# Query projection of a two-head attention step on all 128 rows, and the keys' last tokens as a block diagonal

## The chip, the cores and the metric

The kernel runs as one program on one core of a Trainium2 chip. The metric is the device time of one execution in microseconds (us). A difference of up to 0.2% (2.9 us) between two kernels is about what a measurement of this kernel can't tell from no change.

## What is computed

Three stages follow one another. The first is an attention with a feature map: `phi` projects queries and keys with one 64x128 matrix, subtracts the largest absolute value of the row, and takes `exp` of plus and of minus the result.

```
def phi(x):
    proj = np.einsum('bhsd,df->bhsf', x, w_phi)
    proj = proj - np.max(np.abs(proj), axis=-1, keepdims=True)
    return np.concatenate([np.exp(proj), np.exp(-proj)], axis=-1)
q_p, k_p = (phi(q), phi(k))
kv = np.einsum('bhsf,bhsd->bhfd', k_p, v)
z = np.sum(k_p, axis=2)
num = np.einsum('bhsf,bhfd->bhsd', q_p, kv)
den = np.einsum('bhsf,bhf->bhs', q_p, z)[..., None] + 1e-06
return (num / den).astype(np.float32)
```

There are 4 batches, 8 heads, 576 tokens and 64 numbers per head. The second stage is `g @ w_out` with `g = h - tanh(h)` and `h = x @ w_in` (2304 tokens, 512 to 2048 to 512). The third adds four experts, `out += p[:, e] * (relu(x @ w1[e]) @ w2[e])`, 512 to 1024 to 512.

## The kernel before, in words

**Split numbers.** Most large products take each fp32 operand as a high and a low part of type fp32r. `split3` (L371 holds its matmul) issues three matmuls for each product: high by high, high by low and low by high.

**Order.** For the first two stages nothing is issued directly. `add` (class `Issue`) records a node with an engine, an assumed duration, the nodes that it waits for, the buffers and PSUM banks that it takes, and a due time. `Issue.run` then plays these nodes through once, with the assumed durations, and issues them in the order that comes out. A node's assumed duration, its buffers and its banks therefore decide where its instructions, and those of its neighbours, stand on each engine. On the chip every engine works through its own list in order. The third stage is in an order written by hand.

**Attention tasks.** Two heads are worked on together: head 0 of the pair lies on partitions 0 to 63, head 1 on 64 to 127. There are 16 key tasks (`k_task`: 4 batches by 4 pairs) and 32 query tasks (`q_task`: each with half of the tokens, N = 288). They lie in the first 410 us or so, mixed with the second stage's blocks (`moe_slot`, `moe_x2`) of 288 tokens.

**Query task.** Three transposes (L541) bring 288 tokens of both heads into one PSUM bank. ScalarE copies that to the high part `qh` (L544), VectorE subtracts to the low part `ql` (L545). Then six matmuls (L555) project: for each of three pairs of weight and data (`wph` by `qh`, `wph` by `ql`, `wpl` by `qh`) one matmul for each head. Each uses 64 rows of the array; the two heads' matmuls of a pair write different banks. `wph` and `wpl` hold the 64x128 matrix twice, one copy under the other.

**Key task.** Four transposes (L428) and one more for the last 64 tokens (L431, from `krawr`, of which only partitions 0 to 63 hold data). ScalarE copies 512 tokens to `kT` (L434), VectorE the last 64 tokens (L436). Eight fp32 matmuls on 64 rows project the 512 tokens (L447), and two fp32 matmuls on 64 rows and 64 columns (`mmr`, L465) the last ones. L497, L501 and L507 are the products of key features with `v` and with ones; they write 64 partitions at a time.

**Names used later.** L581 transposes a query task's projection (`pq`) for the maximum, L597 multiplies its exponentials by `kv`, L612 transposes its result. L511 transposes a key task's sums. L648 to L653 are the second stage's activation. L319 to L328 convert the second stage's weights from 64-bit words.

## Time and profile before

| what | value |
|---|---|
| median of three executions | 1437.89 us (1437.07 to 1438.95) |
| span of the profiled execution, first to last instruction | 1435.3 us |
| TensorE busy / its weight loads | 98% / 89% of the span |
| VectorE, ScalarE, GpSimd busy | 75%, 47%, 47% |
| mean granted TensorE clock | 0.995 |

The span is 2.6 us under the median of the executions; what lies around it is start and end of the program. "PE" is TensorE's matmuls and "PEld" its weight loads, "DVE" VectorE, "ACT" ScalarE, "POOL" GpSimd, "SP" the engine whose queue issues the loads and stores. Matmuls are pipelined: one matmul of 288 columns is shown as some 0.29 us long, while the next starts 0.13 us after it. What a matmul takes from TensorE is the distance from its start to the start of the next; a busy share near 100% hides gaps shorter than that overlap.

### The profile page before, as it was taken

To read this page: it belongs to the slowest core of one execution; us is meant where nothing else is said; L and a number is where in the kernel's file an instruction comes from. 1 tells how busy PE (TensorE), PEld (TensorE's weight loads), DVE (VectorE), ACT (ScalarE), POOL (GpSimd) and SP (SyncE) were. 2 spreads that over 40 slices of the span, in tenths; PEclk is the share of its full clock that TensorE was granted. 3 is DMA by queue.
4 is the path that set the end of the run, shared out by engine and by line. 5 is a ranking of instruction groups with operands and counts; after the bars stand their busy time and mean duration, and the time that the engine had idled before them with its cause. 6 is when DMAs were issued, how large, how long until landed. Compare 5 with 4: busy or idle time off the path is not lost.

```text
span 1435.3 us, 24190 instructions
## 1 busy us (share of the span) xinstructions
PE 1401.6 (98%) x9088; PEld 1278.5 (89%) x9088; DVE 1074.9 (75%) x1943; ACT 677.8 (47%) x1639; POOL 677.8 (47%) x567
## 2 busy tenths in 40 slices
PE   8988999999999999999999999999999999999998
PEld 6777888989999999999889999898999989999997
DVE  5898578888867866766777777877777788777774
ACT  6756566666656655564433333433333343333331
POOL 2786354554414322254545544654454466445441
PEclk9999999999999999999999999999999999999999
DMA  6531225443414333212232121233222123221211
GB/s 175 168 114 56 83 88 153 131 131 105 136 52 165 118 132 111 93 74 88 78 103 74 59 73 62 71 118 97 72 67 74 60 74 111 66 73 60 74 44 44
DMA packets 118339, 133.77 MB, mean 93 GB/s; under 512 B 49232, under 2 KB 90320, under 8 KB 118224
## 3 DMA queue, kind: packets, MB, share of 16 engines
q1 hardware_dynamic: 118064, 132.18, 28.7%
q8 instruction: 71, 1.16, 0.3%
q14 instruction: 44, 0.36, 0.1%
q10 hardware_dynamic: 160, 0.07, 0.0%
HBM read 104.44 MB, written 27.79 MB: 92 GB/s over the span
## 4 chain that ended last, share of the span: by engine, by line
PE 83%; DVE 6%; POOL 3%; issue 3%; ACT 3%; DMA 1%; SPq 1%; POOLq 0%; DVEq 0%; ACTq 0%
PE acc L371 36%; PE bank L371 35%; PE bank L597 3%; PE bank L497 1%; POOL wslot L328 1%; PE bank L581 1%; PE bank L555 1%; DVE hs L650 1%; PE acc L497 1%; DVE xc L992 1%; PE bank L447 1%; PE acc L507 1%; DMA xq<-x2f 1%; DVE th L652 0%; DVE wtmp L814 0%
## 5 line engine op out<-in xcount | busy, mean ns | idle before, releaser
L818 POOL TENSOR_TENSOR wslot<-wtmp,wslot 128x512 fp32r<-128x512 f32 x96 | 124.3, 1295 | 268.9 <-ACT wslot L816 166.3
L371 PE MATMUL acc<-gh,wslot 128*128 128x288 f32 x1024 | 240.5, 304 | 3.2 <-ACT gh L653 3.0
L371 PEld LDWEIGHTS acc<-gh,wslot 128*128 128x128 f32 x1024 | 174.7, 189 | 8.1 <-issue 4.0
L964 POOL TENSOR_TENSOR wslot<-raw,wslot 128x512 fp32r<-128x512 f32 x96 | 137.7, 1454 | 91.2 <-ACT wslot L964 88.6
L246 POOL TENSOR_TENSOR gl<-th,gh 128x288 fp32r<-128x288 f32 x92 | 81.2, 883 | 180.0 <-ACT gh L653 151.0
L371 PE MATMUL acc<-gl,wslot 128*128 128x288 f32 x512 | 151.8, 296 | 1.0 <-POOL gl L246 1.0
L652 DVE COPY_PREDICATED th<-sq,hs 128x288 f32<-128x288 int32 x128 | 86.5, 677 | 47.4 <-ACT sq L651 47.2
L371 PE MATMUL bank<-xt0h,wslot 128*128 128x288 f32 x496 | 112.0, 301 | 4.0 <-POOL wslot L328 2.4
L371 PE MATMUL bank<-xt1h,wslot 128*128 128x288 f32 x512 | 114.0, 298 | 0.2 <-DVE kd L454 0.2
L818 POOL TENSOR_TENSOR wslot<-raw,wslot 128x512 fp32r<-128x512 f32 x96 | 109.0, 1154 | 4.4 <-ACT wslot L816 4.4
L992 DVE TENSOR_TENSOR xc<-bank,xc 128x384 f32<-128x384 f32 x168 | 92.2, 549 | 11.6 <-PE bank L371 11.6
L992 DVE TENSOR_TENSOR xc<-acc,xc 128x384 f32<-128x384 f32 x168 | 92.1, 549 | 11.3 <-PE acc L371 10.6
L371 PEld LDWEIGHTS acc<-gl,wslot 128*128 128x128 f32 x512 | 97.0, 189 | 1.2 <-POOL gl L246 1.2
L814 DVE TENSOR_TENSOR wtmp<-raw 128x256 f32<-128x256 f32 x96 | 96.8, 1008 | 0.0
L651 ACT ACTIVATE sq<-sq,b_m 128x288 f32<-128x288 f32 x128 | 69.0, 540 | 47.9 <-DVE hs L650 45.6
L371 PEld LDWEIGHTS bank<-xt0h,wslot 128*128 128x128 f32 x496 | 83.5, 189 | 6.1 <-POOL wslot L328 3.3
L648 DVE SCALAR_TENSOR_TENSOR hs<-bank,sq 128x288 f32<-128x288 f32 x126 | 57.0, 453 | 41.9 <-ACT th L647 40.7
L653 ACT ACTIVATE gh<-th 128x288 fp32r<-128x288 f32 x128 | 57.4, 448 | 62.8 <-PE acc L371 37.5
L371 PEld LDWEIGHTS bank<-xt1h,wslot 128*128 128x128 f32 x512 | 86.0, 189 | 1.1 <-DVE kd L454 0.4
L646 ACT ACTIVATE sq<-bank 128x288 f32<-128x288 f32 x126 | 51.8, 411 | 61.9 <-PE bank L371 59.8
L650 DVE SCALAR_TENSOR_TENSOR hs<-sq,hs 128x288 f32<-128x288 f32 x128 | 76.6, 599 | 0.0
L371 PE MATMUL bank<-xt1l,wslot 128*128 128x288 f32 x256 | 75.8, 296 | 0.0
(397 smaller groups left out, 4097.1 us busy)
## 6 DMA issues: line engine op xcount, KB each, us to landing
raw<-in_moe_w_dram SPq DMA_DIRECT2D x96, 512.0 KB, 3.6
raw<-in_moe_w_in_dram SPq DMA_DIRECT2D x16, 512.0 KB, 4.4
raw<-in_moe_w_out_dram SPq DMA_DIRECT2D x16, 512.0 KB, 5.3
qraw<-in_q_dram SPq DMA_DIRECT2D x32, 144.0 KB, 2.9
x2s<-x2p SPq DMA_DIRECT2D x8, 576.0 KB, 3.3
x2p<-x2s SPq DMA_DIRECT2D x8, 576.0 KB, 6.2
x2f<-x2p SPq DMA_DIRECT2D x8, 576.0 KB, 2.8
out_dram<-yacc SPq DMA_DIRECT2D x18, 256.0 KB, 2.1
```

Source lines behind the costliest of these rows:

```text
L246: return add("POOL", c_pool(n), lambda: POOL.tensor_tensor(out=o, in0=a, in1=b, op=op), deps, due, bufs)
L371: PE.matmul(ps, lhsT=a, rhs=b, start=start and n == 1, stop=stop and n == 3 * len(pairs))
L646: x1 = add("ACT", c_act(N, True), lambda: ACT.activation(out=sq.t, in_=at(bk)[:, 0:N], func=ACTF.Square), [a], due, [sq], frees=[bk])
L648: y1 = add("DVE", c_dve(N), lambda: DVE.scalar_tensor_tensor(out=hs.t, in0=at(bk)[:, 0:N], scalar=P1, in1=sq.t, op0=ALU.mult, op1=ALU.mult ...
L650: y3 = add("DVE", c_dve(N), lambda: DVE.scalar_tensor_tensor(out=hs.t, in0=sq.t, scalar=P0 / P1, in1=hs.t, op0=ALU.add, op1=ALU.mult), [y1 ...
L651: x3 = add("ACT", c_act(N, ptr=True), lambda: ACT.activation(out=sq.t, in_=sq.t, func=ACTF.Relu, scale=-1.0, bias=b_m[:, 0:1]), [y3], due ...
L652: y4 = add("DVE", c_dve(N), lambda: DVE.copy_predicated(out=th.t, mask=sq.t.bitcast(I32), data=hs.t), [x3, y2, y3], due + 1.4, [th, sq, hs])
L653: x4 = add("ACT", c_act(N), lambda: ACT.activation(out=gh.t, in_=th.t, func=ACTF.Copy), [y4], due + 2, [th, gh])
L814: steps = [("DVE", 0.36, lambda o=o, a=a, b=b, op=op: DVE.tensor_tensor(out=o, in0=a, in1=b, op=op)) for o, a, b, op in sums]
L818: steps.append(("POOL", c_pool(n), lambda h=h, l=l, src=src: POOL.tensor_tensor(out=l, in0=src, in1=f32(h), op=ALU.subtract)))
L964: todo2 = [lambda c=c: (ACT.activation(out=vh[:, c], in_=r2[:, c], func=ACTF.Copy), POOL.tensor_tensor(out=vl[:, c], in0=r2[:, c], in1=f32 ...
L992: DVE.tensor_tensor(out=o, in0=bk, in1=a, op=ALU.add)
```

## The change

Each head of the query task now has its own 128-row operand: on one half of the partitions its high part, on the other half its low part. Two matmuls on all 128 rows for each head (with `wph`, then `wpl`, accumulated) give four terms, low by low among them. The copy and the subtraction are done for each head apart, on 64 partitions of output, and each head's projection is a node of its own with one bank. In the key task, the last 64 tokens of the two heads are loaded by two transfers into the diagonal blocks of `krawr`, so that one fp32 matmul on 128 rows by 128 columns projects both; the transposed block has a buffer of its own, `kTr`.

```diff
-        DVE.memset(t[64:128], 0.0)
+        DVE.memset(t[0:64, 1], 0.0)
+        DVE.memset(t[64:128, 0], 0.0)
...
-    kT_r = ring(att, 1, [128, S], F32, "kT")
+    kT_r = ring(att, 1, [128, 512], F32, "kT")
+    kTr_r = ring(att, 1, [128, 128], F32, "kTr")
...
-    qh_r = ring(att, 2, [128, N], F32R, "qh")
-    ql_r = ring(att, 2, [128, N], F32R, "ql")
+    qx_r = ring(att, 2, [128, 2, N], F32R, "qx")
...
-            (rrb.t[0:64], k[b, h:h + 2, 512:S, :].rearrange("h p d -> p h d")),
+            (rrb.t[0:64, 0], k[b, h, 512:S, :]),
+            (rrb.t[64:128, 1], k[b, h + 1, 512:S, :]),
...
-        a2 = add("DVE", c_dve(64), lambda: DVE.tensor_copy(out=kT.t[:, 512:S], in_=at(bb)[:, 0:64]), [a], t0 + 0.6, [kT], frees=[bb])
+        a2 = add("DVE", c_dve(128), lambda: DVE.tensor_copy(out=kTr.t, in_=at(bb)[:, 0:128]), [a], t0 + 0.6, [kTr], frees=[bb])
...
-            for e in range(2):
-                h0 = 64 * e
-                PE.matmul(at(bk)[h0:h0 + 64, 0:128], lhsT=kT.t[h0:h0 + 64, 512:S], rhs=wphi[h0:h0 + 64, :], start=True, stop=True)
+            PE.matmul(at(bk)[:, 0:128], lhsT=kTr.t, rhs=wphi, start=True, stop=True)
...
-        a = add("PE", 0.41, mmr, [a2], due, [kT, kdr], bank=bk)
+        a = add("PE", 0.3, mmr, [a2], due, [kTr, kdr], bank=bk)
...
-        a1 = add("ACT", c_act(N, True), lambda: ACT.activation(out=qh.t, in_=at(bk)[:, 0:N], func=ACTF.Copy), [a], t0 + 0.5, [qh], frees=[bk])
-        a1 = add("DVE", c_dve(N), lambda: DVE.tensor_tensor(out=ql.t, in0=at(bk)[:, 0:N], in1=f32(qh.t), op=ALU.subtract), [a1], t0 + 0.9, [qh, ql], frees=[bk])
...
-        def proj():
-            for n, (w, x) in enumerate(((wph, qh), (wph, ql), (wpl, qh))):
-                for e in range(2):
-                    h0 = 64 * e
-                    PE.matmul(at(pb[e])[:, 0:N], lhsT=w[h0:h0 + 64, :], rhs=x.t[h0:h0 + 64, :], start=n == 0, stop=n == 2)
-
-        a = add("PE", 0.42, proj, [a1], t0 + 1.4, [qh, ql, pq, ea, eb], banks=pb)
+        pj = []
+        for e in range(2):
+            own, other = slice(64 * e, 64 * e + 64), slice(64 - 64 * e, 128 - 64 * e)
+
+            def proj(e=e):
+                for n, w in enumerate((wph, wpl)):
+                    PE.matmul(at(pb[e])[:, 0:N], lhsT=w, rhs=qx.t[:, e], start=n == 0, stop=n == 1)
+
+            a = add("ACT", c_act(N, True), lambda e=e, own=own: ACT.activation(out=qx.t[own, e], in_=at(bk)[own, 0:N], func=ACTF.Copy), [tr_done], t0 + 0.5, [qx], frees=[bk])
+            a = add("DVE", c_dve(N), lambda e=e, own=own, other=other: DVE.tensor_tensor(out=qx.t[other, e], in0=at(bk)[own, 0:N], in1=f32(qx.t[own, e]), op=ALU.subtract), [a], t0 + 0.9, [qx], frees=[bk])
+            pj.append(add("PE", 0.28, proj, [a], t0 + 1.4, [qx, pq, ea, eb], bank=pb[e]))
```

The copy of the projection (`pq`) and the exponentials then wait for their own head's projection instead of for both.

**How the order moves, TensorE in the steady part.** This is the last query task, about 409 us into the run before, between two products of the second stage (`bank<-xt...` is the first layer, `acc<-g...` the second). Before:

```order
L371 MATMUL bank_87<-xt0l,wslot_126 128x288
L371 MATMUL bank_87<-xt0h,wslot_126 128x288
L555 MATMUL bank_86<-qh_217,wph 128x288
L555 MATMUL bank_85<-qh_217,wph 128x288
L555 MATMUL bank_86<-ql_219,wph 128x288
L555 MATMUL bank_85<-ql_219,wph 128x288
L555 MATMUL bank_86<-qh_217,wpl 128x288
L555 MATMUL bank_85<-qh_217,wpl 128x288
L371 MATMUL acc_80<-gh_257,wslot_131 128x288
L371 MATMUL acc_80<-gl_261,wslot_131 128x288
```

The same place on TensorE after the change (L613 is the transpose that was L612):

```order
L371 MATMUL bank_85<-xt0l,wslot_126 128x288
L371 MATMUL bank_85<-xt0h,wslot_126 128x288
L554 MATMUL bank_87<-qx_220,wph 128x288
L554 MATMUL bank_87<-qx_220,wpl 128x288
L371 MATMUL acc_80<-gh_258,wslot_131 128x288
L371 MATMUL acc_80<-gl_262,wslot_131 128x288
L371 MATMUL acc_80<-gh_258,wslot_131 128x288
L613 MATMUL bank_86<-ident,xf_235 128x96 x3
L554 MATMUL bank_84<-qx_220,wph 128x288
L554 MATMUL bank_84<-qx_220,wpl 128x288
L371 MATMUL acc_81<-gh_258,wslot_131 128x288
```

Six matmuls in one piece became two pieces of two, one for each head, with other work between them.

**VectorE at the start.** The first key and query task, 6 to 10 us into the run. Before (L453 and L454 are the keys' maximum and its subtraction):

```order
L378 MEMSET krawr_190 64x128
L378 MEMSET krawr_191 64x128
L436 COPY kT_196<-acc_82 128x64
L545 TENSOR_TENSOR ql_218<-acc_81,qh_216 128x288
L453 TENSOR_REDUCE km_200<-acc_83 128x4
L453 TENSOR_REDUCE km_200<-acc_80 128x4
```

After the change (L455 is the maximum that was L453):

```order
L378 MEMSET krawr_191 64x64
L379 MEMSET krawr_191 64x64
L438 COPY kTr_199<-acc_82 128x128
L557 TENSOR_TENSOR qx_219<-acc_81,qx_219 64x288 x2
L455 TENSOR_REDUCE km_203<-acc_83 128x4
L455 TENSOR_REDUCE km_203<-acc_80 128x4
```

Ahead of the first maximum stand two subtractions in place of one, and a copy of twice the width.

**TensorE at the start.** The stretch before the first product of keys and `v` (L497), 10 to 14 us into the run. Before:

```order
L581 MATMUL bank_87<-ident,pq_220 96x128 x3
L581 MATMUL acc_82<-ident,pq_220 96x128 x3
L431 MATMUL acc_83<-ident,krawr_191 128x128
L541 MATMUL acc_81<-ident,qraw_194 128x96 x3
L497 MATMUL acc_80<-kp_202,vbuf_98 64x256
```

After (the rows L449, the second key task's projection, come eight times in all):

```order
L541 MATMUL acc_82<-ident,qraw_197 128x96 x3
L582 MATMUL bank_87<-ident,pq_221 96x128 x3
L433 MATMUL acc_81<-ident,krawr_191 128x128
L449 MATMUL acc_83<-wphi,kT_198 128x128
L449 MATMUL acc_80<-wphi,kT_198 128x128
...
L497 MATMUL acc_81<-kp_205,vbuf_98 64x256
```

The transposes of the third query load no longer stand ahead of L497; the second key task's projection does, which stood behind L507 before.

## Rows read from the trace of the kernel before

**Rows 1.** Windows: stretch, its length, busy of each engine, PEclk, DMA share, GB/s.

```profile
0.00:50.00 50.00, 45.11 (x412) 35.74 (x412) 30.93 (x79) 32.80 (x89) 18.38 (x18) 0.97 0.62 162
50.00:140.00 90.00, 77.62 (x647) 67.55 (x648) 82.31 (x151) 57.70 (x159) 69.15 (x57) 0.96 0.38 113
140.00:410.00 270.00, 267.26 (x2356) 241.84 (x2355) 208.05 (x452) 171.62 (x496) 128.35 (x125) 1.00 0.36 111
120.00:125.00 5.00, 3.15 (x12) 2.94 (x13) 5.00 (x9) 1.68 (x3) 2.79 (x3) 0.73 0.02 5
500.00:650.00 150.00, 150.00 (x1131) 150.00 (x1130) 102.56 (x217) 81.67 (x192) 49.09 (x50) 1.00 0.27 98
```

**Rows 2.** Chain that ended last, shares by line: 50 to 140, then 140 to 410 us.

```profile
by line: issue 14.2%; PE bank L371 8.2%; POOL wtmp L319 5.8%; POOL gl L246 5.8%; DVE th L652 4.2%; POOL wslot L328 4.1%; DVE hs L650 4.0%; DVE kd L454 3.5%; DVE km L453 3.4%; PE acc L371 3.3%; PE acc L497 2.7%; POOL xf L607 2.6%; PE acc L50
...
by line: PE acc L371 22.6%; PE bank L371 19.5%; PE bank L597 16.0%; PE bank L497 7.7%; PE bank L581 4.6%; PE bank L555 4.2%; PE bank L447 3.3%; DVE hs L650 2.2%; PE bank L612 1.9%; PE bank L541 1.9%; PE bank L511 1.6%; PE bank L501 1.4%; PE
```

**Rows 3.** Timeline of PE at 409 us: start, length, engine, line, op, tiles, form, count.

```profile
409.00 0.29 PE L371 MATMUL bank<-xt0h,wslot 128*128 128x288 f32 x1
409.22 0.40 PE L555 MATMUL bank<-qh,wph 64*128 64x288 f32 x2
409.45 0.29 PE L555 MATMUL bank<-ql,wph 64*128 64x288 f32 x2
409.59 0.29 PE L555 MATMUL bank<-qh,wpl 64*128 64x288 f32 x2
409.81 0.40 PE L371 MATMUL acc<-gh,wslot 128*128 128x288 f32 x1
410.05 0.29 PE L371 MATMUL acc<-gl,wslot 128*128 128x288 f32 x1
```

**Rows 4.** Timeline of PE at 113 us: transposes between two L371.

```profile
112.73 0.30 PE L371 MATMUL acc<-gh,wslot 128*128 128x288 f32 x1
112.86 0.41 PE L541 MATMUL bank<-ident,qraw 96*128 96x96 f32 x3
113.06 0.38 PE L371 MATMUL acc<-gh,wslot 128*128 128x288 f32 x1
113.28 0.29 PE L371 MATMUL acc<-gl,wslot 128*128 128x288 f32 x1
```

**Rows 5.** Chain in order of time: start, us, what, count.

```profile
19.84 1.09 PE acc L447 x16
...
22.11 0.37 PE bank L465 x4
...
33.53 0.44 PE acc L511 x4
...
500.68 1.60 PE bank L371 x12
```

**Rows 6.** Windows, busy (count): VectorE in L545; last row TensorE, loads in L555.

```profile
0.00:50.00 50.00, 2.27 (x5) 0.97 0.62 162
50.00:140.00 90.00, 3.14 (x7) 0.96 0.38 113
140.00:410.00 270.00, 8.80 (x20) 1.00 0.36 111
...
140.00:410.00 270.00, 14.70 (x132) 9.59 (x132) 1.00 0.36 111
```

**Rows 7.** Chain in order of time, near 132 and near 66 us.

```profile
131.96 0.36 DVE xt0l L628
...
65.51 0.60 ACT pq L561 x2
```

**Rows 8.** Timeline of PE near 121 us; in brackets idle time before, releaser.

```profile
120.89 0.40 PE L371 MATMUL acc<-gh,wslot 128*128 128x288 f32 x1 [2.97 <-ACT gh L653]
```

**Rows 9.** Timeline: the SP queue's second load, and PE's wait near 13 us.

```profile
1.54 0.76 SPq L254 DMA_DIRECT2D krawr<-in_k_dram  x1
...
13.55 0.71 PE L541 MATMUL acc<-ident,qraw 96*128 96x96 f32 x3 [2.57 <-DMA qraw<-in_q_dram]
```

More of the change, by code (lines that the diff above doesn't have):

```diff
@@ L422, in k_task @@
         ], due=t0 - 4, bufs=[vb])
-        kT, km = kT_r.take(), km_r.take()
+        kT, kTr, km = kT_r.take(), kTr_r.take(), km_r.take()
         ba, bb = Bank(), Bank()
@@ L434, in k_task @@
         a1 = add("ACT", c_act(512, True), lambda: ACT.activation(out=kT.t[:, 0:512], in_=at(ba), func=ACTF.Copy), [a], t0 + 0.5, [kT], frees=[ba])
-        a = add("PE", 0.1, trr, [ld], t0 + 0.1, [rrb, kT], bank=bb)
-        a2 = add("DVE", c_dve(64), lambda: DVE.tensor_copy(out=kT.t[:, 512:S], in_=at(bb)[:, 0:64]), [a], t0 + 0.6, [kT], frees=[bb])
+        a = add("PE", 0.1, trr, [ld], t0 + 0.1, [rrb, kTr], bank=bb)
+        a2 = add("DVE", c_dve(128), lambda: DVE.tensor_copy(out=kTr.t, in_=at(bb)[:, 0:128]), [a], t0 + 0.6, [kTr], frees=[bb])
         kps, es = [], []
@@ L536, in q_task @@
         ], due=t0 - 8, bufs=[rb])
-        bk, qh, ql = Bank(), qh_r.take(), ql_r.take()
+        bk, qx = Bank(), qx_r.take()
         def tr():
@@ L541, in tr @@
                 PE.transpose(out=at(bk)[:, r * QP:(r + 1) * QP], in_=rb.t[:, r].rearrange("p h d -> p (h d)"), identity=ident[0:QP, 0:QP])
-        a = add("PE", 0.3, tr, [ld], t0, [rb, qh, ql], bank=bk)
-        a1 = add("ACT", c_act(N, True), lambda: ACT.activation(out=qh.t, in_=at(bk)[:, 0:N], func=ACTF.Copy), [a], t0 + 0.5, [qh], frees=[bk])
-        a1 = add("DVE", c_dve(N), lambda: DVE.tensor_tensor(out=ql.t, in0=at(bk)[:, 0:N], in1=f32(qh.t), op=ALU.subtract), [a1], t0 + 0.9, [qh, ql], frees=[bk])
+        tr_done = add("PE", 0.3, tr, [ld], t0, [rb, qx], bank=bk)
         pb = [Bank(), Bank()]
         pq, ea, eb = pq_r.take(), ea_r.take(), eb_r.take()
-        def proj():
-            for n, (w, x) in enumerate(((wph, qh), (wph, ql), (wpl, qh))):
-                for e in range(2):
-                    h0 = 64 * e
-                    PE.matmul(at(pb[e])[:, 0:N], lhsT=w[h0:h0 + 64, :], rhs=x.t[h0:h0 + 64, :], start=n == 0, stop=n == 2)
-        a = add("PE", 0.42, proj, [a1], t0 + 1.4, [qh, ql, pq, ea, eb], banks=pb)
+        pj = []
[7 more added lines that the diff above has]
+            pj.append(add("PE", 0.28, proj, [a], t0 + 1.4, [qx, pq, ea, eb], bank=pb[e]))
         pc, xe = [None, None], []
@@ L560, in copy @@
             def copy(e=e):
-                pc[e] = add("ACT", c_act(N, True), lambda: ACT.activation(out=pq.t[:, e], in_=at(pb[e])[:, 0:N], func=ACTF.Copy), [a], t0 + 2, [pq], frees=[pb[e]])
+                pc[e] = add("ACT", c_act(N, True), lambda: ACT.activation(out=pq.t[:, e], in_=at(pb[e])[:, 0:N], func=ACTF.Copy), [pj[e]], t0 + 2, [pq], frees=[pb[e]])
             def exps(e=e):
                 for x, sg in ((ea, 1.0), (eb, -1.0)):
-                    xe.append(add("ACT", c_act(N, True), lambda x=x, sg=sg: ACT.activation(out=x.t[:, e], in_=at(pb[e])[:, 0:N], func=ACTF.Exp, scale=sg), [a], t0 + 2.4, [x], frees=[pb[e]]))
+                    xe.append(add("ACT", c_act(N, True), lambda x=x, sg=sg: ACT.activation(out=x.t[:, e], in_=at(pb[e])[:, 0:N], func=ACTF.Exp, scale=sg), [pj[e]], t0 + 2.4, [x], frees=[pb[e]]))
             copy()
```

## Prediction
> **What bounds the kernel now.** I read the windows first, since attention, where every edited line runs, lies in the first 410 us. [rows 1] give three regimes. From 140 to 410 us TensorE is busy 267.3 of 270 us, VectorE 208.1 (77%), ScalarE 171.6. From 50 to 140 us VectorE is busy 82.3 of 90 us (91%) and TensorE 77.6. From 0 to 50 us neither is full. From 500 to 650 us, after attention, TensorE is busy all 150 us, so what attention saves is not waited for again there.
>
> The chain of work that ended last says the same by line [rows 2]. From 140 to 410 us it runs along TensorE: the three largest entries are L371, L371 and L597, and the query projection itself (L555) has 4.2%. From 50 to 140 us it is scattered over TensorE, GpSimd, VectorE and 14.2% of time between engines; no line has more than a tenth. So a slot of TensorE saved after 140 us should come back nearly whole; before that it should come back only in part, and VectorE work may cost.
>
> **TensorE: what a query projection takes now.** Not the 0.29 us of a row counts, but the distance between starts. Twelve L371 in a row take 1.60 us [rows 5]: 0.133 us is the plain slot of 288 columns. In [rows 3] the projection's two matmuls of a pair start together (x2 in each row): the two heads do run beside each other. But the group stands out at both ends. From the last L371 to the first pair are 0.22 us in place of 0.133, and from the first to the second pair 0.23 in place of 0.133; the next step is 0.14. On the way back it is 0.22 from the last pair to L371, and 0.24 to the L371 behind. So each passage between whole-array and 64-row matmuls costs about 0.09 at the boundary and 0.10 to 0.11 for weights that are not loaded ahead, 0.197 us together. From 409.00 to 410.05 the group takes 1.05 us, where two slots of L371 would take 0.27: it costs 0.78 us.
>
> Is it the 64-row form that costs, or any change of work? [rows 4] show three transposes (L541) between two L371: they start 0.13 after the L371 ahead, and the L371 behind is followed after 0.22. So whole-array work of another kind has no boundary cost going in, and something like 0.09 coming back from fp32. The projection after the change is fp32r like L371 and uses the whole array, so I take nothing at its ends.
>
> The Trainium skill (TensorEngine Tiling (Array Packing), Key Properties) says that a change of tiling mode drains TensorE, and that tiles work independently. The 0.22 against 0.133 at both ends agrees; the second 0.10 is not in that sentence.
>
> **TensorE: what it takes after.** Four matmuls on 128 rows: 4 x 0.133 = 0.53 us, in one piece or in two. Against 0.78 that is 0.25 less where both neighbours use the whole array. The general count comes from the order: walking down TensorE's whole list, the form changes (all rows; 64 rows; 64 columns, L497 to L507; 64 by 64, L465) 141 times before and 62 times after, 79 fewer. At 0.197 that is 15.6 us; at 0.15, since L465 loads only 64 columns and some neighbours are fp32, 11.9 us. The extra streaming is one slot for each of 32 query tasks (three pairs become four matmuls): 32 x 0.133 = 4.3 us. For L465 [rows 5], four records (two heads, two passes) take 0.37 us with its exit; after the change one fp32 matmul of 128 columns has two passes, by the nearest row (L511, four of 128 columns in 0.44, 0.11 each) 0.22 us. Its streaming is thus unchanged, its switches are in the 79. Sum for TensorE: 11.9 - 4.3 = 7.6 to 15.6 - 4.3 = 11.3 us less; I take 9.5.
>
> Where does it fall? 20 of 32 low-part subtractions (L545) stand after 140 us, 7 between 50 and 140, 5 before [rows 6]. Of the six matmuls of each of 32 tasks, 132 of 192 follow 140 us [rows 6], those of 22 tasks. So 22/32 x 9.5 = 6.5 us are saved where TensorE is the chain; I count it whole. The other 3.0 lie before 140 us.
>
> **VectorE and ScalarE: what is added.** Instead of one subtraction on 128 partitions there are two on 64, each with the same 288 columns. No 64-partition subtraction of this form is in the trace; below, it could take half, above, the whole of a 128-partition one. I take the whole, for what is passed through is columns. In the chain such a subtraction holds VectorE 0.36 us (L628, [rows 7]), so 32 x 0.36 = 11.5 us, of which 20 x 0.36 = 7.2 after 140 us and 7 x 0.36 = 2.5 between 50 and 140. The copy of the keys' last tokens doubles to 128 columns: 64 more at 0.36/288 are 0.08 us each, 1.3 for 16 tasks. ScalarE gets 32 more copies; two of that size take 0.60 in the chain [rows 7], so 32 x 0.30 = 9.6 us.
>
> After 140 us both are covered: VectorE has 62 us idle there, ScalarE 98, and TensorE's own stream is the cover. If that cover is gone in a piece (VectorE full for some 10 us), the subtractions of one or two tasks show, 0.36 to 0.7 us. Between 50 and 140 us VectorE is nearly full, so 2.5 + 6 x 0.08 = 3.0 us can show; bounds 0 and 3.0, and I take 1.8, towards the upper end because 91% is nearer to full than not.
>
> **Latency.** Head 0's operand is ready as before (one copy, one subtraction), head 1's one step of 0.36 later; its TensorE node is apart, so the list can hold other work between them, as the steady place in the order shows. What waits behind a late head 1 is the rest of TensorE's list, but at most 0.36 us.
>
> **The start.** The second `krawr` transfer costs the SP queue about 0.76 us [rows 9] in each key task; ahead of the second query load stand two of them, so it lands some 1.5 us later. Ahead of the first key maximum VectorE gets one more subtraction and two more small memsets, 0.5 to 0.7 us. Against that, before, TensorE stands 2.57 us at the transposes of the third query load [rows 9], and behind them waits L497. In the new order these transposes no longer precede L497; the second key projection (L449, sixteen records, 1.09 us [rows 5]) does, and it is done early. What is late next is L497 itself, for its exponentials. I take 1 us gained by 50 us, between a loss of 1.5 and a gain of 3.
>
> **Sum.** -6.5 (after 140 us) + 1.8 (VectorE, 50 to 140) - 1.0 (start) = -5.7 us. From the span 1435.3 that gives 1429.6, and with the 2.6 us that lie around it 1432.2; the median shown is 1437.9. The forecast is 1432.2 us.
>
> **Rivals.**
>
> *VectorE takes it.* TensorE's saving is real, but in parts of the stretch after 140 us too a block's end waits for VectorE, and only the rest of it pays. For it: the 91%, and `hs` L650 is the only entry of another engine among the first eight of the chain after 140 us. Against: there TensorE idles 2.7 of 270 us. The 6.5 shrink to about 4, all of VectorE's 3.0 shows and the start brings nothing: -1.0, 1436.9 us.
>
> *The pairs were worth more than the switches.* If the 0.197 at the ends is not of the form but of the waits that surround any group, it stays, and the change only turns three slots into four. 4.3 us more on TensorE give 1442.2 us, with VectorE's 3.0 on top 1445.2. It decides as soon as less than 4.3/79 = 0.054 us is saved per switch. Against: the 0.22 is the same where the transposes have none [rows 4]. The Trainium skill speaks for it (TensorEngine Tiling (Array Packing), Theoretical Speedup): a contraction of up to 64 gains up to 2x by row tiles. By that rule alone, without the switches, the time would be the 1442.2 us of this rival; the x2 rows agree that pairs run together, the ends say that the doubling is not what these groups got.
>
> *A long wait in the new order.* Before 140 us the whole list is shuffled. Near 121 us TensorE stands 2.97 us [rows 8], and over 120 to 125 us its granted clock is 0.73 on the mean [rows 1]: part of that stretch ran at the lower level of 1.2 GHz, which costs 0.27 x 5 = 1.35 us more. One event of this kind costs 4.3 us. TensorE's idle time before 140 us is 4.9 + 12.4 = 17.3 us [rows 1], so there is room for the new order to be luckier or unluckier. Two more such events turn the forecast into 1440.8 us; shedding the present one gives 1427.9.
>
> **Chances.** The forecast's mechanism with a gain between 3 and 10 us: 0.57. The same with waits shed too, about 1428: 0.09. VectorE takes it, within 0.2%: 0.20. Pairs worth more: 0.06, slower. Waits in the new order, slower: 0.08. That gives faster 0.66, same 0.20, slower 0.14. The range runs from 1425 (the present event shed, and TensorE's upper sum: 22/32 x 11.3 = 7.8 in place of 6.5, a start of -2.5 in place of -1) to 1440.5 us (nearly two added events); for the forecast alone it is 1428 to 1435.
>
> **What the profile after would show.** L554 in starts 0.13 us apart with 0.13 at both ends if the form is the cause; 0.22 there if it is not. L465 followed by 0.11 steps. In the window that answers to 140 to 410 us, the same second-stage products ending about 6 us earlier with TensorE still near full. VectorE near 0.36 us for each L557, or half of that if partitions count. The prediction is wrong if TensorE's idle time before 140 us grows past 20 us, if more stretches show a clock near 0.7, or if the 64-partition subtraction that writes other partitions than it reads takes much longer than the old one.

## The result and the profile after

The change made the kernel slower: 1451.59 us (median of four, 1450.64 to 1453.92) against 1438.42 us of the kernel before on the same chip (1437.07 to 1439.89). The ratio is 1.0087, 95% interval 1.0073 to 1.0101, some 12.5 us. The forecast was 1432.2 us. The profiled execution has a span of 1449.9 us.

The windows after, which answer to [rows 1] (same columns; the third reaches to 426 us, since attention now ends later, the fourth is a part of the second):

```profile
0.00:50.00 50.00, 44.70 (x400) 38.37 (x402) 34.87 (x86) 34.87 (x95) 14.66 (x17) 0.97 0.58 154
50.00:140.00 90.00, 76.62 (x596) 67.44 (x593) 80.04 (x149) 57.53 (x155) 62.42 (x52) 0.91 0.37 114
140.00:426.00 286.00, 274.25 (x2359) 251.60 (x2358) 227.64 (x487) 188.49 (x540) 131.01 (x130) 1.00 0.34 105
...
69.20:76.20 7.00, 7.00 (x46) 6.65 (x45) 4.68 (x12) 2.69 (x9) 6.03 (x6) 0.51 0.89 289
...
500.00:650.00 150.00, 150.00 (x1131) 150.00 (x1131) 101.14 (x216) 81.88 (x193) 50.14 (x52) 1.00 0.27 98
```

From 500 to 650 us TensorE is as full as before (150 of 150 us). After 140 us TensorE now stands for 286 - 274.25 = 11.8 us, before for 2.7. From 50 to 140 us its mean granted clock is 0.91 where it was 0.96, which is 0.05 x 90 = 4.5 us of its time; from 69.20 to 76.20 us it ran at the lower level (0.51 of full) while it was busy all the time.

A block of the second stage ends with four copies from `acc` to `x2p`. The tile's view (line, count, durations in ns, first and last start in us) of before and of after, for the first six of eight blocks:

```profile
L710 ACT ACTIVATE x2p<-acc x24: 387/452/513, 144.0 to 413.1; 128x288 f32<-128x288 f32 x24
```

```profile
L711 ACT ACTIVATE x2p<-acc x24: 392/412/541, 140.6 to 424.7; 128x288 f32<-128x288 f32 x24
```

The same view for all eight blocks:

```profile
L710 ACT ACTIVATE x2p<-acc x32: 387/430/513, 144.0 to 476.0; 128x288 f32<-128x288 f32 x32
```

```profile
L711 ACT ACTIVATE x2p<-acc x32: 388/412/541, 140.6 to 488.1; 128x288 f32<-128x288 f32 x32
```

The two profiled spans differ by 14.6 us. The sixth block ends 11.6 us later and the eighth 12.1, so most of the loss lies in the stretch with attention. The other 2.5 us fall behind the eighth block, where no edited line runs; there the time differs between the runs below, too, from 959 to 967 us. The first and last start of the six blocks serve for the experiments.

The timeline of TensorE after, at a place where the operand is in time, answers to [rows 3]:

```profile
208.72 0.29 PE L371 MATMUL acc<-gh,wslot 128*128 128x288 f32 x1
208.85 0.29 PE L554 MATMUL bank<-qx,wph 128*128 128x288 f32 x1
208.98 0.29 PE L554 MATMUL bank<-qx,wpl 128*128 128x288 f32 x1
209.12 0.30 PE L371 MATMUL bank<-xt0h,wslot 128*128 128x288 f32 x1
```

Every step is 0.13 us: no boundary, no exposed weights. So the part of the forecast on TensorE's own time holds here. What it did not see is in the waits after 140 us (engine, line, what it waited for, us in total, times, longest):

```profile
PE acc L371 <- ACT x2p L711: 3.0, 2, 2.3
PE bank L554 <- DVE qx L557: 2.8, 3, 1.5
PE bank L433 <- DVE xt1l L629: 1.5, 1, 1.5
PE bank L613 <- DVE qx L557: 1.4, 1, 1.4
```

TensorE waits for the new subtractions (L557), and for copies on ScalarE that stand behind the new ones. Two of these waits, in the timelines of GpSimd, VectorE and TensorE near 348 us, then of VectorE, GpSimd, ScalarE and TensorE near 371 us:

```profile
347.55 0.74 POOL L484 TENSOR_TENSOR ks<-ks,kpr 64x256 f32<-64x256 f32 x1
348.25 1.30 POOL L481 TENSOR_TENSOR tz<-kp 128x512 f32<-128x512 f32 x1
...
347.65 2.24 DVE L653 COPY_PREDICATED th<-sq,hs 128x288 f32<-128x288 int32 x1
349.93 0.46 DVE L557 TENSOR_TENSOR qx<-bank,qx 64x288 fp32r<-64x288 f32 x1
...
350.53 0.44 PE L613 MATMUL bank<-ident,xf 96*128 96x96 f32 x3 [1.42 <-DVE qx L557]
351.02 0.37 PE L554 MATMUL bank<-qx,wph 128*128 128x288 f32 x1
```

```profile
369.06 0.95 DVE L320 TENSOR_SCALAR wtmp<-wtmp 128x512 uint32<-128x512 uint32 x1
...
369.94 2.28 DVE L653 COPY_PREDICATED th<-sq,hs 128x288 f32<-128x288 int32 x1
...
370.57 1.30 POOL L481 TENSOR_TENSOR tz<-kp 128x512 f32<-128x512 f32 x1
...
372.25 0.45 DVE L557 TENSOR_TENSOR qx<-bank,qx 64x288 fp32r<-64x288 f32 x1
...
372.25 0.44 ACT L654 ACTIVATE gh<-th 128x288 fp32r<-128x288 f32 x1 [2.06 <-DVE th L653]
372.74 0.83 ACT L556 ACTIVATE qx<-bank 64x288 fp32r<-64x288 f32 x2
373.47 1.28 ACT L711 ACTIVATE x2p<-acc 128x288 f32<-128x288 f32 x4
...
373.92 0.40 PE L371 MATMUL acc<-gh,wslot 128*128 128x288 f32 x1 [2.29 <-ACT x2p L711]
```

Both begin with L653, which lasts 2.24 and 2.28 us in place of some 0.5 while GpSimd sums key features (L484, L481). Behind it come a subtraction, or ScalarE's list with two new copies in it, and TensorE stands still for 1.42 and 2.29 us.

### The profile page after: what moved, and what is told of

It is laid out like the page before. It is cut to its first block, busy times and chain, and to the rows that moved or that the text cites. A ratio compares the mean times of both kernels' runs of the same rounds, so it can differ in the third digit from the quotient of the medians.

```text
span 1449.9 us, 24098 instructions
## 1 busy us (share of the span) xinstructions
PE 1402.0 (97%) x8992; PEld 1285.1 (89%) x8992; DVE 1094.6 (75%) x1977; ACT 693.1 (48%) x1671; POOL 669.7 (46%) x567
## 4 chain that ended last, share of the span: by engine, by line
PE 81%; DVE 8%; issue 3%; ACT 3%; POOL 2%; DMA 2%; SPq 1%; POOLq 0%; DVEq 0%; ACTq 0%
PE bank L371 35%; PE acc L371 34%; PE bank L598 3%; POOL wslot L328 1%; PE bank L497 1%; PE bank L582 1%; PE bank L554 1%; DVE wtmp L322 1%; DVE hs L651 1%; PE acc L598 1%; PE bank L449 1%; DMA xq<-x2f 1%; DVE xc L993 1%; PE acc L497 1%; DVE th L653 1%
## 5 line engine op out<-in xcount | busy, mean ns | idle before, releaser
L371 PE MATMUL acc<-gh,wslot 128*128 128x288 f32 x1024 | 241.1, 301 | 3.3 <-ACT x2p L711 3.3
L371 PEld LDWEIGHTS acc<-gh,wslot 128*128 128x128 f32 x1024 | 175.0, 188 | 4.5 <-ACT x2p L711 4.3
L371 PE MATMUL acc<-gl,wslot 128*128 128x288 f32 x512 | 151.3, 295 | 1.8 <-POOL gl L246 0.9
L653 DVE COPY_PREDICATED th<-sq,hs 128x288 f32<-128x288 int32 x128 | 87.1, 681 | 49.6 <-ACT sq L652 49.4
L371 PE MATMUL bank<-xt0h,wslot 128*128 128x288 f32 x496 | 113.3, 303 | 6.6 <-POOL wslot L328 4.2
L371 PE MATMUL bank<-xt1h,wslot 128*128 128x288 f32 x512 | 113.5, 296 | 0.3 <-DVE th L650 0.3
L993 DVE TENSOR_TENSOR xc<-bank,xc 128x384 f32<-128x384 f32 x168 | 92.3, 549 | 11.6 <-PE bank L371 11.5
L371 PEld LDWEIGHTS acc<-gl,wslot 128*128 128x128 f32 x512 | 96.5, 189 | 2.7 <-POOL gl L246 1.5
L371 PEld LDWEIGHTS bank<-xt0h,wslot 128*128 128x128 f32 x496 | 84.5, 191 | 9.5 <-POOL wslot L328 5.4
L371 PEld LDWEIGHTS bank<-xt1h,wslot 128*128 128x128 f32 x512 | 85.6, 188 | 0.8 <-DVE th L650 0.5
L371 PE MATMUL bank<-xt1l,wslot 128*128 128x288 f32 x256 | 75.5, 295 | 0.0
## 6 DMA issues: line engine op xcount, KB each, us to landing
qraw<-in_q_dram SPq DMA_DIRECT2D x32, 144.0 KB, 2.9
```

Source lines behind the costliest of these rows:

```text
L371: PE.matmul(ps, lhsT=a, rhs=b, start=start and n == 1, stop=stop and n == 3 * len(pairs))
L653: y4 = add("DVE", c_dve(N), lambda: DVE.copy_predicated(out=th.t, mask=sq.t.bitcast(I32), data=hs.t), [x3, y2, y3], due + 1.4, [th, sq, hs])
L993: DVE.tensor_tensor(out=o, in0=bk, in1=a, op=ALU.add)
```

## Experiments

Four theories were put to the test. **A**: split by heads, the operand's links copy, subtraction, copy, subtraction stand one behind the other, and TensorE waits. **T** (called C in the first expectations): 32 more operations on VectorE and on ScalarE are too much in themselves. **B**: any change of the plan's numbers draws another order, with other waits and other stretches at half clock. **D**: the new passes, or the keys' third transfer, don't pay. Each ratio is to the kernel before on the same chip, with its 95% interval. "Stretch" is the distance from the first `x2p` copy to the last in the tile's view, 413.1 - 144.0 = 269.1 us before; it leaves out what happens ahead of the first copy, and is given where the order is the old one. Both columns come from the one execution that was profiled, whose time is up to some 3 us off the median of its kernel, so a first copy alone that is 2 or 3 us later shows little.

| run | order | ratio (95%) | first copy, stretch |
|---|---|---|---|
| the change | its own | 1.0087 (1.0073 to 1.0101) | - |
| e1 new keys only | its own | 1.0050 (1.0038 to 1.0062) | - |
| e2 new query only | its own | 1.0064 (1.0046 to 1.0082) | - |
| e3 whole change, unsplit | old | 1.0047 (1.0035 to 1.0060) | 147.4, 272.2 |
| e5 whole change, unsplit | its own | 1.0031 (1.0019 to 1.0042) | - |
| e6 before | e5's | 0.9998 (0.9988 to 1.0007) | - |
| e7 passes only | old | 1.0003 (0.9990 to 1.0015) | 148.1, 264.2 |
| e8 work only | old | 1.0054 (1.0038 to 1.0070) | 145.1, 276.8 |
| e9 before | e1's | 1.0042 (1.0029 to 1.0056) | - |
| e10 work, not waited for | old | 1.0026 (1.0017 to 1.0035) | 145.4, 273.0 |
| e11 subtraction only | old | 1.0050 (1.0038 to 1.0063) | 147.5, 276.5 |
| e12 new keys only | old | 1.0004 (0.9995 to 1.0013) | 146.0, 267.4 |
| e14 the change, copies first | the change's | 1.0069 (1.0056 to 1.0081) | - |
| e15 before, no sums | old | 0.9940 (0.9927 to 0.9952) | 139.8, 265.1 |
| e16 work only, no sums | old | 0.9965 (0.9953 to 0.9977) | 144.0, 268.1 |
| e17 whole change, no sums | old | 0.9962 (0.9949 to 0.9974) | 144.8, 263.6 |
| e18 new keys, third load moved | old | 0.9989 (0.9980 to 0.9997) | 146.8, 267.4 |
| e19 whole change, chained | old | 1.0120 (1.0102 to 1.0137) | 151.5, 277.0 |
| e20 e18, key copy on ScalarE | old | 0.9994 (0.9984 to 1.0003) | 148.8, 267.1 |

"Old order" means that nodes and assumed durations are those of before and that only what a node issues differs, so that on every engine the instructions stand in the old order. (In e19 the second copy is issued with the subtractions, and so stands later in ScalarE's list; in e20 a copy changes its engine.)

**e1 and e2: the halves of the change.** e1 takes the parts of the diff on `krawr`, `kT`, `kTr` and `mmr`, e2 the parts on `qx`.

> The block diagonal of the keys' last tokens alone; the query projection is the old one. Theory A (the time was lost in the query step: its links copy, subtraction, copy, subtraction stand one behind the other, so that TensorE waits for head 1): the keys' part is free of that, so 1434 to 1438 us (16 groups of two 64-row matmuls become one whole-array pair of passes, at most 16 x 0.2 = 3.2 us less TensorE, part of it before 140 us where VectorE bounds). Theory B (any change of the planner's numbers reshuffles the order of the first 140 us, and it is the order that loses or wins): the order changes here too, so a time off the kernel before by more than 4 us either way is likely. Theory C (the additional copies and subtractions are too much for ScalarE and VectorE): none here, as A.

> The query projection of the change, split by heads, with the old keys. Theory A: most of the loss is here, 1444 to 1452 us. Theory B: yet another order, anywhere from 1434 to 1452, with idle time before 140 us and half clock that set it.

1447.93 and 1449.48 us: each half alone loses, and the two losses do not add up. Theory A had said that the keys alone are free of the loss, and it missed; e1 is off by more than 4 us, as theory B had it, and e2 fits both. That called for a fixed order.

**e3, e5 and e6: one node for both heads, in the old order and in its own; the old instructions in the latter.**

```diff
+        def halves():
+            for e in range(2):
+                own = slice(64 * e, 64 * e + 64)
+                ACT.activation(out=qx.t[own, e], in_=at(bk)[own, 0:N], func=ACTF.Copy)
...
-        a1 = add("ACT", c_act(N, True), lambda: ACT.activation(out=qh.t, in_=at(bk)[:, 0:N], func=ACTF.Copy), [a], t0 + 0.5, [qh], frees=[bk])
+        a1 = add("ACT", c_act(N, True), halves, [a], t0 + 0.5, [qx], frees=[bk])
```

(the subtractions and the four matmuls alike; e5 with `2 * c_act`, `2 * c_dve` and 0.56.)

> The instructions of the whole change (block-diagonal keys, stacked operands, four whole-array query matmuls), but a pair's two copies are one step of the plan, its two subtractions one step and its four matmuls one step, with the plan's durations as before: the order on every engine is that of the kernel before. Theory A: the links copy, subtraction, copy, subtraction are gone (both copies first, then both subtractions), head 1 comes some 0.8 us later than before (one copy 0.39, one subtraction 0.45) and most places have that slack: 1429 to 1436 us. Theory B: the order is the old one, so the old idle time stays and the saving on TensorE shows: 1429 to 1433. Theory C: the work is all here, so the loss stays: 1445 to 1452.

> As the kernel with the old order, but the plan knows the true durations (two copies, two subtractions, 0.56 us of matmuls, 0.3 us of key matmul), so the order is a new one. Theory A: no chain from head to head, 1429 to 1436 us. Theory B: another draw of the order, anywhere from 1428 to 1452, and not the time of the kernel with the old order. Theory C: 1445 to 1452.

> The instructions of the kernel before (64-row matmuls, one copy, one subtraction) in exactly the order of the unsplit kernel with true durations. Theory B: the order sets the time, so it differs from the kernel before by as much as the unsplit kernel does, give or take the 5 to 9 us of TensorE that the instructions are worth. Theory A: the order alone costs little, 1436 to 1441 us. Theory C: 1436 to 1441 us, and 8 us or more faster than the unsplit kernel, since the additional work is left out.

1446.71, 1445.63 and 1439.49 us. Theories A (1429 to 1436 us) and B (1429 to 1433) missed e3, and A missed e5. With the order held the instructions still lose 0.47%; in another order they lose about 0.33% (1.0031 against 0.9998), and that order is worth nothing by itself, against theory B. So the loss is not only the order's, and it is there without a split by heads.

**e7, e8, e11: the parts of e3 apart.** e7 has the whole-array passes and leaves out the additional work, so each head's matmuls read high parts or low parts of both heads; e8 has the additional work with the old matmuls (the copies are cut like the subtractions shown); e11 is as e8 with the copy whole.

```diff
 # e7
-            for e in range(2):
-                own = slice(64 * e, 64 * e + 64)
-                ACT.activation(out=qx.t[own, e], in_=at(bk)[own, 0:N], func=ACTF.Copy)
+            ACT.activation(out=qx.t[:, 0], in_=at(bk)[:, 0:N], func=ACTF.Copy)
 # e8
-            DVE.tensor_tensor(out=ql.t, in0=at(bk)[:, 0:N], in1=f32(qh.t), op=ALU.subtract)
+            for e in range(2):
+                own = slice(64 * e, 64 * e + 64)
+                DVE.tensor_tensor(out=ql.t[own], in0=at(bk)[own, 0:N], in1=f32(qh.t[own]), op=ALU.subtract)
```

> Old order. Keys as a block diagonal and four whole-array query matmuls, but the operand is left wrong: one copy and one subtraction over all 128 rows as before, the first head's matmuls read the low parts of both heads and the second head's the high parts, so the output is not the reference's. What is left out is only the additional work of ScalarE and VectorE. Theory A (the second copy and the second subtraction make the operand late, and TensorE waits): the saving on TensorE shows once they are gone, 1432 to 1436 us. Theory D (the passes save TensorE next to nothing, since the old pairs cost 0.68 us between neighbours and the new four 0.53, and the third transfer of the keys takes the rest back): 1437 to 1441. Theory B (order): 1432 to 1436, as A.

> Old order, old keys, old 64-row matmuls; only the copy and the subtraction of a query step are cut in two of 64 partitions each, as in the change (same rows in and out, output unchanged). Theory A: this alone loses what the kernel with the old order lost and the saving on TensorE as well: 1444 to 1449 us. Theory D and theory B: hidden behind TensorE's own stream, 1438 to 1442.

> The kernel before in its own order; only the subtraction is cut in two of 64 partitions, the copy stays whole. If VectorE is what loses: 1443 to 1448 us. If the two copies on ScalarE do: 1438 to 1441 us.

1440.45, 1447.09 and 1447.14 us. The work alone loses as much as e3, and the second subtraction alone as much as the work: it is VectorE. The passes gain nothing in the whole time, but they do on TensorE. TensorE's timeline of e7 at the place of [rows 3]:

```profile
408.42 0.30 PE L371 MATMUL bank<-xt0h,wslot 128*128 128x288 f32 x1
408.55 0.29 PE L559 MATMUL bank<-qx,wph 128*128 128x288 f32 x1
...
408.94 0.29 PE L559 MATMUL bank<-qx,wpl 128*128 128x288 f32 x1
409.08 0.30 PE L371 MATMUL acc<-gh,wslot 128*128 128x288 f32 x1
409.21 0.29 PE L371 MATMUL acc<-gl,wslot 128*128 128x288 f32 x1
```

From 408.42 to 409.21 are 0.79 us where there were 1.05: the forecast 0.25 per group. The stretch is shorter by 4.9 us. The windows of e7 show part of what takes it back:

```profile
0.00:50.00 50.00, 42.98 (x374) 34.34 (x375) 28.48 (x74) 29.98 (x81) 17.38 (x17) 0.93 0.61 162
50.00:140.00 90.00, 77.56 (x630) 69.46 (x628) 82.73 (x152) 56.31 (x153) 66.89 (x53) 0.92 0.37 113
```

The clock is 0.93 and 0.92 where [rows 1] have 0.97 and 0.96, 0.04 x 140 = 5.6 us of TensorE's time, part of it hidden behind VectorE; the first `x2p` copy comes 4.1 us later. Another 3.4 us lie behind the sixth block (1437.9 - 412.3 against 1435.3 - 413.1 us), where nothing was changed. Over all 12 executions of e7 the mean granted clock is 0.992, where the kernel before beside them had 0.994; but e12 below, with the old query projection, has 0.992 as well. Theory D had the time right. Its first half, that the passes save next to nothing, was wrong; its second, that the third transfer of the keys takes the saving back, e12 and e18 bear out in part.

**e10: the same work where nobody waits for it.** Copy and subtraction stay whole; behind each comes one more of 64 partitions.

```diff
+            ACT.activation(out=spare[0:64], in_=at(bk)[0:64, 0:N], func=ACTF.Copy)
...
+            DVE.tensor_tensor(out=spare[64:128], in0=at(bk)[64:128, 0:N], in1=f32(qh.t[64:128]), op=ALU.subtract)
```

> The kernel before in its own order, with the change's additional work placed so that no matmul waits for it: behind each whole copy ScalarE makes a copy of 64 partitions, behind each whole subtraction VectorE makes one of 64 partitions, into a spare tile (bfloat16 out, read by nobody). Theory L (lateness: the second subtraction stands between the operand and the matmuls): 1438 to 1442 us. Theory T (throughput: 32 more operations of 0.4 us on each of two in-order queues push everything behind them back, whoever waits): 1444 to 1449 us, as the kernel in which the matmuls do wait for them.

1443.64 us, between what theory L and theory T had: the stretch grows by 3.9 us, in e8 by 7.7. About half of the loss is lateness of the operand, half that VectorE's list is pushed back. How a 0.46 us operation pushes more than itself shows near 308 us. VectorE of the kernel before, and then VectorE, GpSimd and TensorE of e10:

```profile
306.00 0.45 DVE L545 TENSOR_TENSOR ql<-bank,qh 128x288 fp32r<-128x288 f32 x1
306.37 0.86 DVE L321 SCALAR_TENSOR_TENSOR wtmp<-raw,wtmp 128x512 uint32<-128x512 uint32 x1
307.15 0.45 DVE L648 SCALAR_TENSOR_TENSOR hs<-bank,sq 128x288 f32<-128x288 f32 x1
```

```profile
308.05 0.46 DVE L552 TENSOR_TENSOR spare<-bank,qh 64x288 bf16<-64x288 f32 x1
308.54 2.36 DVE L321 SCALAR_TENSOR_TENSOR wtmp<-raw,wtmp 128x512 uint32<-128x512 uint32 x1
...
309.05 1.30 POOL L482 TENSOR_TENSOR tz<-kp 128x512 f32<-128x512 f32 x1
...
311.30 0.45 DVE L660 TENSOR_TENSOR th<-bank,th 128x288 f32<-128x288 f32 x1
...
311.80 0.40 PE L566 MATMUL bank<-qh,wph 64*128 64x288 f32 x1 [1.43 <-DVE th L660]
```

GpSimd's sums run there in both kernels (before from 304.19 to 310.82 us). Pushed back by one operation, L321 falls differently among them: it outlasts the long sum L482 (to 310.35) and takes 2.36 us in place of 0.86. L660 behind it frees the bank that TensorE needs. A window of the kernel before shows that there was no room for the operation, whatever the mean of 77% said (VectorE is the third busy time):

```profile
300.00:311.00 11.00, 10.54 (x82) 9.63 (x82) 10.97 (x20) 7.12 (x20) 7.71 (x7) 1.00 0.19 53
```

**e15, e16, e17: the same without GpSimd's sums.** The sums of `tz`, `ks` and `kpr` are left out; the tile that they would fill holds ones. e15 is the kernel before, e16 has the work of e8, e17 the whole change as in e3.

```diff
-                POOL.tensor_tensor(out=tz.t.rearrange("p j f -> p (j f)"), in0=kp.t[:, 0:2].rearrange("p j a f -> p (j a f)"), in1=kp.t[:, 2:4].rearrange("p j a f -> p (j a f)"), op=ALU.add)
+                pass
```

> The kernel before in its own order without GpSimd's sums over the key features (the 24 sums tz, ks and ks with kpr; the sums' tile holds ones, so the denominators and the output are not the reference's). It is the base for the two kernels below. Stretch theory (operations of VectorE that meet these sums last 2 us in place of 0.5 to 1): 1432 to 1439 us, little less than before since the old order covers most of the stretched ones.

> As the kernel without sums, with the copy and the subtraction of a query step cut in two of 64 partitions each (the same left out). Stretch theory (the additional work loses 7 us because it moves VectorE's chain into the sums, where an operation that TensorE waits for is stretched): at most 3 us above the kernel without sums. Theory T (VectorE is short of time whatever GpSimd does): 6 to 8 us above it, as with the sums.

> The instructions of the whole change in the old order, without GpSimd's sums (the same left out). Stretch theory: the passes' saving on TensorE shows, 0 to 5 us below the kernel without sums. Theory T: 4 to 7 us above it.

1430.95, 1435.40 and 1434.90 us. Without the sums the kernel before gains 0.60%, more than the little that was expected: they already cost it time. The work costs 0.25% here (0.9965 against 0.9940) where it cost 0.54%, so neither theory has it alone. After the first copy it is clearer: 3.0 us (268.1 against 265.1) in place of 7.7, and TensorE hardly waits; this is the window of e16, with 1.1 us of idle TensorE and VectorE less full than in [rows 1] in spite of the work:

```profile
140.00:410.00 270.00, 268.87 (x2363) 244.06 (x2362) 206.65 (x476) 180.79 (x519) 70.96 (x69) 1.00 0.36 110
```

The rest of its loss lies ahead of 144 us (first copy at 144.0 against 139.8). In e17 the passes take 4.5 us off the stretch again (263.6 against 268.1). Even so e17 is 0.22% slower than e15, where the stretch theory had it at or below: its stretch is 1.5 us shorter, its first copy 5.0 us later. And leaving the sums out shortens GpSimd's own list too, so these runs do not show that the collision alone makes the difference.

**e9 and e12: what the new keys lose.** e9 has the old instructions in e1's order, e12 the new keys in the old order.

> The instructions of the kernel before in exactly the order of the kernel with the new keys alone. Theory B (the order and the half clock that its early waits bring lost the 8 us of that kernel): 1444 to 1449 us. Theory D (its third transfer and the block diagonal themselves lost it): 1438 to 1442.

> The block diagonal of the keys alone, in the order of the kernel before (the plan reckons with the old durations). Theory B (the 8 us of the new keys in their own order were the order's): 1436 to 1441 us: 16 x 0.13 = 2 us less TensorE, 1.2 us later first query tile behind the third transfer. Theory D (the block diagonal itself loses): 1444 to 1448 us.

1445.38 and 1441.17 us. The order that the planner drew for e1 loses 0.42% with the old instructions in it; in the old order the new keys are worth nothing that can be measured. Theory B holds for this order, and e6 shows one where it doesn't. For e12 theory B had 1436 to 1441 us, so the saving on TensorE that it counted on did not show; e18 says more.

**e14 and e19: the split.** e14 issues both copies in the first head's place; e19 puts the chain of the change into the old order of e3.

```diff
 # e19, in the node of the subtractions
                 own, other = slice(64 * e, 64 * e + 64), slice(64 - 64 * e, 128 - 64 * e)
+                if e:
+                    ACT.activation(out=qx.t[own, e], in_=at(bk)[own, 0:N], func=ACTF.Copy)
```

> The change itself, in its own order, but ScalarE makes both heads' copies in the first head's place, so that the second copy no longer waits for the first subtraction. Theory A (the chain copy, subtraction, copy, subtraction makes head 1 late, beyond the work itself): 3 to 6 us less than the change, 1444 to 1449 us. Theory T or B: as the change, 1449 to 1454 us.

> The instructions of the whole change in the old order, but the second head's copy stands behind the first head's subtraction and waits for it, as in the change (VectorE's two subtractions still stand next to each other). Theory A (the chain copy, subtraction, copy, subtraction costs beside the work): 3 to 8 us more than the same kernel with both copies first (1446.7 against 1440.0 of before), so 1449 to 1455 us. If the chain costs nothing: 1445 to 1449 us, and what the change has above that is its own order's.

1450.45 and 1457.84 us. In the old order the chain costs 0.73% beyond e3, more than theory A had said. ScalarE waits for VectorE in 24 of the 32 query steps, and VectorE for the second copy in all of them, as the waits of e19 say:

```profile
ACT qx L550 <- DVE qx L551: 16.9, 24, 2.8
DVE qx L551 <- ACT qx L550: 19.0, 32, 1.6
```

In the change itself, where other work often stands between the two subtractions, cutting the chain gives 0.18%, with intervals that overlap; theory A had 3 to 6 us there, and its upper end of 1449 us was missed. So the chain can cost more than everything else, but how much of the change's loss it is stays open.

**e18 and e20: towards a faster kernel.** e18 is e12 with the additional load of the first key task on ScalarE's queue; e20 also copies `kTr` on ScalarE.

```diff
 # e18
-                SP.dma_start(out=o, in_=i)
+                eng = ACT if count and not len(started) and o is pairs[-1][0] else SP
+                eng.dma_start(out=o, in_=i)
 # e20
-DVE.tensor_copy(out=kTr.t, in_=at(bb)[:, 0:128])
+ACT.activation(out=kTr.t, in_=at(bb)[:, 0:128], func=ACTF.Copy)
```

> The block diagonal of the keys alone, in the old order, and the additional transfer of the first pair's last keys goes over ScalarE's queue and no longer stands ahead of the first query tile on SyncE's. If the 1.2 us of later start is what takes back the keys' saving: 1437 to 1439 us against 1440 before. If the stretch before 140 us takes it (VectorE bound, half clock): 1439 to 1442.

> As the kernel with the new keys in the old order whose third transfer goes over ScalarE's queue (1438.6 us against 1440.6 of before), with the copy of the transposed last keys on ScalarE in place of VectorE: 16 x 0.25 = 4 us less VectorE. By the price of VectorE's time that nobody waits for (14.7 us cost 3.8 us, 0.26 each): 1 us less, 1437 to 1439 us. If ScalarE's queue makes the copy late: 1439 to 1443 us.

e18 takes 1438.63 us against 1440.61 of before, ratio 0.9989 (0.9980 to 0.9997): the only version that still does all of the work and whose interval lies below the kernel before, by less than a measurement is said to tell. Against e12 it differs in the queue of one transfer. That is worth 0.15%, some 2 us, with intervals that just overlap, and the mean granted clock over all executions is 0.995 in place of 0.992 (the kernel before beside either has 0.994). So the place of the additional load, ahead of the second query load, is likely a cost of its own in the change. Taking 4 us from VectorE on top (e20, 1438.24 against 1438.26) shows no gain.

## Why the prediction was wrong

**What bounds the kernel.** Right for TensorE after 140 us, but the sentence on VectorE rested on a mean over 270 us. Behind the 77% stand windows like the one from 300 us, where VectorE is busy 10.97 of 11 us.

**TensorE.** Right in mechanism and size. Add up TensorE's distances from start to start as far as the last transposes of attention, without gaps above 0.03 us and without what half clock added: 395.9 us before, 386.4 in e7, which is 9.5 less. The forecast had 7.6 to 11.3 and took 9.5; that it hits to the tenth is luck. In the stretch e7 kept 4.9 of the 6.5 that were counted whole.

**VectorE and ScalarE: the step that failed.** "After 140 us both are covered ... TensorE's own stream is the cover", with 0.36 to 0.7 us where VectorE is full. The size of a subtraction was right (columns count, not partitions: L557 has a mean of 455 ns after, L545 440 before). The cover was not there: the second subtraction alone costs 0.50% (e11), and e8 loses 7.7 us in the stretch, more than the 6.5 that the passes were to save. About half of that is the late operand, half the list (e10); without GpSimd's sums 3.0 us are left (e16). The text named the condition, VectorE full for some 10 us, but priced it at one or two operations and not at the 1.4 to 2.3 us for which TensorE then stands still.

**Latency.** "At most 0.36 us" failed too. In the plan the bank and the operand, which both engines use, pass from one engine to the other, so head 1's copy waits for head 0's subtraction and its own subtraction comes after that: head 1 is two more steps behind head 0, with the waits between the queues, and not one. Even with both copies first TensorE is paced by VectorE. In e3, TensorE's timeline has the second head 0.34 us behind the last pass of the first, where 0.13 would do:

```profile
405.27 0.29 PE L563 MATMUL bank<-qx,wpl 128*128 128x288 f32 x1
405.61 0.37 PE L563 MATMUL bank<-qx,wph 128*128 128x288 f32 x1
```

**The start.** Not gained. The additional load brings the transposes of the second query load from 9.30 to 10.56 us in e7, near the 1.5 that the forecast had. In the change the first L497 does start earlier, at 13.20 in place of 14.19 us, as expected; but at 20.63 us TensorE has waited 1.90 us for ScalarE, and by 50 us it has been idle for 5.3 us where it was 4.9.

**Rivals.** "VectorE takes it" named the right engine at a wrong price: it let the 6.5 us shrink to 4 and added 3.0 ahead of 140 us, while behind 140 us more than the whole saving was lost. "Pairs worth more" fell with e7. The "long wait in the new order" came too: 0.05 of clock from 50 to 140 us is 4.5 us, about one of the two added events of that rival; it had 0.08. Of the forecast's signs of being wrong one came, stretches at a low clock; the idle time ahead of 140 us, 18.7 us, stayed under its 20, and the new subtraction is no longer than the old one.

**The sum.** From first row to last the change has 9.1 us more idle TensorE after 140 us (11.8 - 2.7), 1.4 more before (18.7 - 17.3 us), and 4.5 us of clock: 15.0 us. The sixth block ends 11.6 us later, so 3.4 us of the saving on TensorE are left. The count of TensorE's distances above agrees: it gives 392.8 us for the change, 3.1 less than before. The rest of the 9.5 presumably went into waits inside its groups, like the one just shown; their sum was not measured. Shown by runs: that VectorE's second subtraction costs as much as the passes save and more, that the work costs less without the sums, and that an order alone can cost 0.4%. Likely, but with intervals that just overlap: that the additional load costs some 2 us (e12 against e18). The old-order kernel with the whole change loses 0.47% (e3), the change 0.87%. How the other 0.4% divide between the chain and the change's own order, with its stretches at the lower clock, stays open.

## What to carry to other kernels

An engine that is 77% busy on the mean covers nothing in a stretch where it is full: before counting added work as hidden, read the windows of some 10 us around the places where it will stand, and the operations behind it in its list. Where a planner sets the order, hold the order and change the instructions, then hold the instructions and change the order; otherwise one measures a draw. A saving on the bounding engine can be worth nothing if the operand now takes longer to make than the matmuls that use it.

## What the hardware showed

Operations of VectorE whose operands all lie in SBUF often last longer while GpSimd's sums run; those that read a PSUM bank don't. The groups of VectorE in the kernel before, from 140 to 410 us (count, busy us, mean ns, idle time before):

```profile
L650 DVE SCALAR_TENSOR_TENSOR hs<-sq,hs 128x288 f32<-128x288 f32 x40 | 25.8, 646 | 0.0
L652 DVE COPY_PREDICATED th<-sq,hs 128x288 f32<-128x288 int32 x40 | 24.1, 602 | 7.7 <-ACT sq L651 7.5
...
L648 DVE SCALAR_TENSOR_TENSOR hs<-bank,sq 128x288 f32<-128x288 f32 x40 | 18.1, 452 | 12.4 <-ACT th L647 11.8
L649 DVE TENSOR_TENSOR th<-bank,th 128x288 f32<-128x288 f32 x40 | 17.8, 446 | 0.0
```

Without the sums (e15) the first two fall to these means, and the two that read a bank stay at 453 and 447 ns:

```profile
L654 DVE COPY_PREDICATED th<-sq,hs 128x288 f32<-128x288 int32 x41 | 21.7, 529 | 11.6 <-ACT sq L653 11.3
L652 DVE SCALAR_TENSOR_TENSOR hs<-sq,hs 128x288 f32<-128x288 f32 x40 | 19.9, 498 | 0.0
```

The Trainium skill (SBUF — State Buffer, Who interferes with whom) says of the ports that VectorE shares with GpSimd: "it's an exclusive lock". By it, an operation of VectorE with two SBUF inputs contends with a GpSimd instruction that reads SBUF, and one with at most one SBUF input does not, unless it runs in a mode that uses both of VectorE's ports. The four rows agree, and the rule, read before the forecast, would have pointed at the copy that is L653 after the change. L320 has one SBUF input and stretches as well: after the change it takes 0.42 us away from GpSimd's work and 0.95 us at 369.06, beside two sums. Which mode it runs in no run here shows.

TensorE's clock fell to its lower level behind a wait. In TensorE's timeline after:

```profile
67.90 0.51 PE L582 MATMUL bank<-ident,pq 128*96 128x128 f32 x3 [2.37 <-DVE qm L585]
```

Then the window from 69.20 to 76.20 us has 0.51, though TensorE was busy for all 7.00 us of it. In e7, with less work on TensorE, more of the first 140 us ran so. That the smaller work is the reason is not shown: e12, with the old query projection, has the same mean clock over its executions (0.992), and moving one load (e18) brings 0.995.
